# Loading input weights as whole rows, u by another queue, and a filter turned by TensorE

## The chip, the cores and the metric

The kernel runs on one core of a Trainium2 chip. A core has five engines that run side by side, each through its own list of instructions in order: PE (TensorE, matmuls, with PEld for its weight loads), DVE (VectorE), ACT (ScalarE), POOL (GpSimd) and SP (SyncE, which here only issues DMAs). Sixteen DMA engines move data. The metric is the device time of one execution in microseconds (us).

## The reference

```python
for t in range(S):                       # r, k, v, w: batch 4, heads 8, S = 768, D = 48
    cur = einsum('bhd,bhe->bhde', u[None] * kt, vt)
    y[:, :, t] = einsum('bhd,bhde->bhe', rt, state + cur)
    state = wt[:, :, :, None] * state + einsum('bhd,bhe->bhde', kt, vt)
x = y as [batch, S, 384]
h = maximum(x @ w_in, 0)                 # w_in 384 x 1024, float64
conv_out[t] = sum_k conv_w[k] * h[t + k - 1]
out = (h * sigmoid(conv_out)) @ w_out    # w_out 1024 x 384, float64
```

w_in, conv_w and w_out are given in float64. [...]

## The kernel before

**Two halves.** The recurrence is computed in 24 chunks of 128 time steps (six for each batch). For a chunk, `stage_a` loads w, k, r and v (1024 runs of 192 bytes each), turns them with PE, forms running products of w with two scans on DVE (L549 and L556), and `stage_b` makes scores on PE (L660), masks them on DVE (L664), adds the carried state and writes a slice of x (`xT`) as a high and a low part. Chunks below `EARLY` = 4 move their last rows with selecting matmuls (`gather`, L569), later ones with small DMAs (L577). The second half, `block`, takes 384 time steps: 8 tiles of x @ w_in (L753, nine matmuls each), the filter and the sigmoid (`gating`), and the product with w_out (L782).

**Weights.** A slot of raw words is loaded into a tile `gh` and converted piece by piece by `convert`: four DVE instructions (`from_double`, L436, L441, L444, L447), with an ACT activation (L439) between the first and the second, a POOL product (L450), an ACT cast to the high part (L456) and a POOL subtraction for the low part (L457). A slot of w_in is a third of the columns of all three row groups: `win_pieces` (L472, L476) fills 48 and 16 partitions at a time, from runs of 3 KB or 2 KB. The filter conv_w is loaded as 3072 runs of 8 bytes, so that each channel lies in its partition. u is one row, loaded by SP behind the first four loads, spread over the partitions by a matmul with ones (L509) and copied into `ubc` by ACT.

**Order.** All of it is written as operations with an engine, a rank, the buffers they hold and a length (`LEN`, `moves`). `Plan.issue` plays these lengths through and writes each engine's instructions in the order that comes out; on the chip every engine then follows its list strictly. `Kind` says how many of the eight PSUM banks a use may hold (`pa` turned inputs and picked rows, `pb` scores and states, `mm` and `mo` the two products, `wx` conversion). Ahead of the plan stand some instructions in code order: `WARM` matmuls on a tile `junk`, memsets, tables.

Of the kernel before, what the change touches and what calls it, by code (L numbers as in the profile page):

```python
# [12 lines left out]
I32 = mybir.dt.int32  # L13
# [8 lines left out]
GH = 5  # L22
WARM = 10

CHUNK, LEAD, UNIT, DOWN, PIECE = 14.0, 0.0, 5.0, 1.6, 4.0
FIRST_IN, FIRST_OUT = 10.0, 60.0
AHEAD, GUARD = 10.0, 10.0
SPREAD = (3, 5)
EARLY = 4
COLD = 60.0  # L30


# [264 lines left out]
def rwkv_conv_moe_kernel(  # L297
# [36 lines left out]


    junk = fconst.tile([P, H, D], BF16, name="junk")
    nc.vector.memset(junk, 0.0)
    idle = junk.rearrange("p h d -> p (h d)")
    for _ in range(WARM):
# [48 lines left out]
    store = (list(banks), [])  # L388
    pa, pb, mm, mo, wx = Kind(3, store, 1), Kind(5, store, 2), Kind(3, store, 1), Kind(3, store, 1), Kind(4, store, 1)

# [18 lines left out]
    g_k = kind("g", 2, [P, HB])  # L409
    wide = ([fconst.tile([P, HB], F32, name=f"wide{i}") for i in range(4)], [])  # L410
    val_k, e_k = Kind(3, wide, 1), Kind(2, wide, 1)
# [10 lines left out]

    def from_double(raw, val, n, reads, writes):

        e, x, y = Buf(e_k), Buf(wx), Buf(wx)

        def exps():
            return x.t.bitcast(I32)[:, 0:n]

        def mant():  # L430
            return y.t.bitcast(I32)[:, 0:n]
# [28 lines left out]
    def load_conv():  # L460
        raw = Buf(conv_k)
        op("SP", "issue", lambda: nc.sync.dma_start(
            out=raw.t.rearrange("p (j t w) -> p j t w", j=3, w=2),
            in_=conv_w.rearrange("j (t p w) -> p j t w", p=P, w=2)), [], [(raw, 0)], [raw], moves=0.2)
        from_double(lambda: raw.t, lambda: cw.rearrange("p j t -> p (j t)"), 3 * FT, [raw, (raw, 0)], ["cw"])

    def win_pieces(f0, n, piece):

        raw = Buf(raw_k)
        cs = slice(2 * f0, 2 * (f0 + n))  # L470
        for g in range(2):
# [4 lines left out]
            op("SP", "issue", lambda g=g: nc.sync.dma_start(  # L476
                out=raw.t[64 * g + D:64 * g + 64, :, 0:2 * n],
                in_=w_in[(6 + g) * D:(7 + g) * D, cs].rearrange("(m i) c -> i m c", m=KT)), [], [(raw, 2 * g + 1)], [raw],
                moves=2.3 * n / 1024)
# [17 lines left out]
    def loads(n):  # L497
# [29 lines left out]
    def stage_a(n):  # L527
# [319 lines left out]
    for t0 in range(0, FT, 3):  # L847
        plan.rank = FIRST_OUT + PIECE * t0
        wout_pieces(t0, min(3, FT - t0), piece)
    blocks = [(b, s0) for b in range(B) for s0 in range(0, S, HB)]  # L850
    bi = 0
    for n in range(N + 1):
        if n < N:
            plan.rank = CHUNK * n - LEAD - AHEAD
            loads(n)
            plan.rank = CHUNK * n - LEAD
            stage_a(n)
            plan.rank = CHUNK * (n + 0.5) - LEAD
            stage_b(n)
# [50 lines left out]
```

## Time and profile before

| | us |
|---|---|
| median of 3 runs (lowest, highest) | 385.2 (384.16, 385.79) |
| the profiled execution | 383.74 |
| its span, first to last instruction | 382.0 |
| PE busy | 353.0 (92%) |
| DVE busy | 285.7 (75%) |
| ACT busy | 234.9 (61%) |
| POOL busy | 174.3 (46%) |

All rows further down are of the profiled execution. Its own time is 1.7 us above its span, and 1.5 us below the median. A busy share is a mean over the whole span; the stages differ, so the rows give them apart.

### The profile page before, as it was taken

The numbers are of one execution on the slowest core, as the hardware profiler recorded it, in microseconds if no ns is written. First come the engines' busy times: TensorE is split into PE (matmuls) and PEld (weight loads), VectorE is DVE, ScalarE is ACT, GpSimd is POOL, SyncE is SP. The second block draws the span as 40 slices with busy tenths as digits, with TensorE's granted clock in tenths as the row PEclk, the third lists the DMA queues.
The fourth block names the chain that finished last, engine by engine and source line by source line (L and its number), as shares of the span: only waits on it lengthen the run. The fifth ranks groups of instructions, "written<-read, shape, count | busy, mean of one in ns | idle before, by whom it ended". The sixth has DMA issues, their size and how long they took to land.

```text
span 382.0 us, 7869 instructions
## 1 busy us (share of the span) xinstructions
PE 353.0 (92%) x2794; PEld 322.2 (84%) x2794; DVE 285.7 (75%) x575; ACT 234.9 (61%) x612; POOL 174.3 (46%) x199
## 2 busy tenths in 40 slices
PE   6839578898899999999999999999999999999994
PEld 3728557787699999998999989998999998999993
DVE  1668999999987986778787786768879755863640
ACT  5145646898766763498648652696775625765741
POOL 5536758857854343066533450373543410332430
PEclk9977698999999999999999999999999999999998
DMA  8989993524433443543343253824334121010001
GB/s 162 129 151 172 267 241 82 115 50 79 82 75 69 100 102 53 133 98 82 74 92 85 55 106 75 165 51 99 78 85 82 33 51 57 0 44 21 22 22 66
DMA packets 116623, 34.44 MB, mean 90 GB/s; under 512 B 106146, under 2 KB 113827, under 8 KB 116579
## 3 DMA queue, kind: packets, MB, share of 16 engines
q1 hardware_dynamic: 116578, 33.89, 43.0%
q8 instruction: 23, 0.38, 0.4%
q14 instruction: 22, 0.17, 0.2%
HBM read 25.19 MB, written 4.72 MB: 78 GB/s over the span
## 4 chain that ended last, share of the span: by engine, by line
PE 73%; DVE 14%; DMA 3%; issue 3%; SPq 2%; POOL 2%; ACT 1%; DVEq 0%; POOLq 0%
PE bank L782 26%; PE bank L753 24%; PE bank L660 5%; PE bank L542 5%; PE bank L726 5%; PE bank L716 4%; DMA gh<-in_moe_w_in_dram 2%; PE bank L677 2%; PE bank L595 2%; SPq L502 1%; DVE kr L549 1%; DVE kr L556 1%; DVE wide L447 1%; DVE bank L444 1%; DVE bank L436 1%
## 5 line engine op out<-in xcount | busy, mean ns | idle before, releaser
L753 PE MATMUL bank<-xT,wi 128*128 128x386 f32 x576 | 124.5, 346 | 0.0
L782 PE MATMUL bank<-wo,gh 128*128 128x384 f32 x576 | 123.3, 343 | 0.0
L775 POOL TENSOR_TENSOR gh<-g,gh 128x384 fp32r<-128x384 f32 x64 | 64.5, 1013 | 111.3 <-ACT gh L774 105.9
L753 PEld LDWEIGHTS bank<-xT,wi 128*128 128x128 f32 x576 | 100.3, 189 | 2.9 <-issue 2.2
L782 PEld LDWEIGHTS bank<-wo,gh 128*128 128x128 f32 x576 | 99.5, 188 | 1.7 <-issue 0.9
L767 DVE SCALAR_TENSOR_TENSOR a<-bank,cw,a 128x384 f32<-128x384 f32 x64 | 38.2, 609 | 22.6 <-ACT a L766 22.6
L587 POOL TENSOR_SCALAR_AFFINE_SELECT pm<-dg 128x1024 f32<-128x1024 f32 x24 | 26.4, 1099 | 51.0 <-PE bank L726 44.8
L771 ACT ACTIVATE a<-a 128x384 f32<-128x384 f32 x64 | 33.4, 523 | 21.9 <-DVE a L769 21.7
L772 DVE TENSOR_TENSOR g<-bank,a 128x384 f32<-128x384 f32 x64 | 34.6, 547 | 11.3 <-ACT a L771 10.6
L765 ACT ACTIVATE bank<-bank 128x386 f32<-128x386 f32 x64 | 30.4, 476 | 20.3 <-PE bank L753 19.0
L664 DVE COPY_PREDICATED pm<-upper,bank 128x512 f32<-128x512 int32 x48 | 33.3, 726 | 10.5 <-PE bank L660 10.3
L769 DVE SCALAR_TENSOR_TENSOR a<-bank,cw,a 128x384 f32<-128x384 f32 x64 | 38.2, 609 | 0.6
L774 ACT CAST gh<-g 128x384 fp32r<-128x384 f32 x64 | 32.3, 511 | 9.7 <-DVE g L772 9.4
L766 ACT ACTIVATE a<-bank,cw 128x384 f32<-128x384 f32 x64 | 36.2, 579 | 0.4
L549 DVE TENSOR_TENSOR_SCAN kr<-bank,one_end 128x387 f32<-128x387 f32 x24 | 23.0, 957 | 15.9 <-PE bank L542 15.8
L581 POOL TENSOR_TENSOR z<-r,k 128x384 f32<-128x384 f32 x24 | 24.3, 1012 | 14.0 <-DMA r<-in_r_dram 14.0
L583 POOL TENSOR_TENSOR z<-z,ubc 128x384 f32<-128x384 f32 x24 | 24.3, 1011 | 4.3 <-ACT ubc L511 3.2
L660 PEld LDWEIGHTS bank<-kr 48*128 48x128 f32 x288 | 19.9, 202 | 6.7 <-issue 4.6
L660 PE MATMUL bank<-kr 48*128 48x128 f32 x288 | 24.7, 305 | 0.4 <-DVE g L772 0.4
L812 ACT COPY wide<-bank 128x384 f32<-128x384 f32 x24 | 11.5, 480 | 21.9 <-PE bank L782 21.4
L569 PE MATMUL bank<-kr,sel 128*112 128x130 f32 x48 | 10.9, 386 | 14.2 <-DVE kr L554 7.0
L556 DVE TENSOR_TENSOR_SCAN kr<-bank,dA 128x387 f32<-128x387 f32 x24 | 22.8, 952 | 0.0
(106 smaller groups left out, 542.2 us busy)
## 6 DMA issues: line engine op xcount, KB each, us to landing
w<-in_w_dram SPq DMA_DIRECT2D x24, 192.0 KB, 3.4
k<-in_k_dram SPq DMA_DIRECT2D x24, 192.0 KB, 3.5
r<-in_r_dram SPq DMA_DIRECT2D x24, 192.0 KB, 3.8
v<-in_v_dram SPq DMA_DIRECT2D x24, 192.0 KB, 3.5
out_dram<-wide SPq DMA_DIRECT2D x24, 192.0 KB, 2.0
gh<-in_moe_w_out_dram SPq DMA_DIRECT2D x2, 1152.0 KB, 9.2
last<-kr SPq DMA_DIRECT2D x120, 16.2 KB, 1.8
gh<-in_moe_w_in_dram SPq DMA_DIRECT2D x4, 432.0 KB, 7.2
```

Source lines behind the costliest of these rows:

```text
L660: nc.tensor.matmul(sc[g].t[:, m * L:(m + 1) * L], lhsT=kt(m)[p], rhs=rt(m)[p], start=True, stop=True)
L664: op("DVE", "cp", lambda g=g: nc.vector.copy_predicated(out=pm.t[:, g], mask=upper.unsqueeze(1).to_broadcast([P, NP, L]), data=sc[g].t.rea ...
L753: nc.tensor.matmul(t.t[:, 0:HB + 2], lhsT=wi[:, m, a, f * P:(f + 1) * P], rhs=xT[:, x0 + m, c, xs], start=(m == 0 and j == 0), stop=(m == ...
L765: ("ACT", "relu", lambda: nc.scalar.activation(out=h(0, width + 2), in_=h(0, width + 2), func=AF.Relu), [t], [t]),
L766: ("ACT", "mul", lambda: nc.scalar.mul(out=a(), in_=h(1), mul=cw[:, 1, bass.ds(f, 1)]), [t, "cw"], [a1]),
L767: ("DVE", "stt", lambda: nc.vector.scalar_tensor_tensor(out=a(), in0=h(0), scalar=cw[:, 0, bass.ds(f, 1)], in1=a(), op0=ALU.mult, op1=ALU. ...
L769: ("DVE", "stt", lambda: nc.vector.scalar_tensor_tensor(out=a(), in0=h(2), scalar=cw[:, 2, bass.ds(f, 1)], in1=a(), op0=ALU.mult, op1=ALU. ...
L771: ("ACT", "sig", lambda: nc.scalar.activation(out=a(), in_=a(), func=AF.Sigmoid), [], [a1]),
L772: ("DVE", "gate", lambda: nc.vector.tensor_tensor(out=g.t[:, 0:width], in0=h(1), in1=a(), op=ALU.mult), [t, a1], [g]),
L774: ("ACT", "cast", lambda: nc.scalar.copy(out=part(0)[:, 0:width], in_=g.t[:, 0:width]), [g], [key]),
L775: ("POOL", "lo", lambda: nc.gpsimd.tensor_tensor(out=part(1)[:, 0:width], in0=g.t[:, 0:width], in1=part(0)[:, 0:width].bitcast(F32), op=AL ...
L782: nc.tensor.matmul(acc.t[:, 0:DM], lhsT=part(a)[:, tt * P:(tt + 1) * P], rhs=wo[:, f, c, :], start=(f == 0 and a + c == 0), stop=(f == FT ...
```

## The change

The change does several things at once:

- u is loaded by ACT's queue as its first instruction, into a fixed tile, and its matmul stands in code order behind the junk matmuls, of which there are 5 and no longer 10. The copy into `ubc` stands in chunk 0's `stage_a`.
- A slot of w_in is one row group `m` with all 1024 columns: 128 whole rows of 8 KB, again to 48 and 16 partitions at a time, cut into pieces of 384, 384 and 256 columns for `convert`. The slots are written among the chunks' operations (slot n behind `stage_a(n)`), as are the slots of w_out.
- The filter is loaded as 24 rows of 1 KB, converted in 24 partitions, turned by one PE transpose and copied into `cw` by ACT.
- `pa` may hold 4 banks instead of 3; the picked rows and the turned keys of the first four chunks go to `pb`. Planning lengths of the weight loads and the ranks of the pieces change.

```diff
-WARM = 10
-
-CHUNK, LEAD, UNIT, DOWN, PIECE = 14.0, 0.0, 5.0, 1.6, 4.0
+WARM = 5
+
+CHUNK, LEAD, UNIT, DOWN, PIECE = 14.0, 0.0, 5.0, 1.6, 5.0
...
+CAPS = (4, 5, 3, 3, 4)
+GT, TB = 1, 1
+WIN = 2.0
...
+    wide = ([fconst.tile([P, HB], F32, name=f"wide{i}") for i in range(4)], [])
+    nc.scalar.dma_start(out=wide[0][0][0:1, :], in_=u.rearrange("h d -> (h d)").unsqueeze(0))
...
     ubc = fconst.tile([P, H, D], F32, name="ubc")
+    nc.tensor.matmul(banks[-1][:, 0:H * D], lhsT=ones_f[0:1, :], rhs=wide[0][0][0:1, :], start=True, stop=True)
...
-    pa, pb, mm, mo, wx = Kind(3, store, 1), Kind(5, store, 2), Kind(3, store, 1), Kind(3, store, 1), Kind(4, store, 1)
+    pa, pb, mm, mo, wx = (Kind(cap, store, keep) for cap, keep in zip(CAPS, (1, 2, 1, 1, 1)))
...
     def load_conv():
-        raw = Buf(conv_k)
+
+        rows = 3 * FT
+        raw, val, t = Buf(e_k), Buf(val_k), Buf(wx)
         op("SP", "issue", lambda: nc.sync.dma_start(
-            out=raw.t.rearrange("p (j t w) -> p j t w", j=3, w=2),
-            in_=conv_w.rearrange("j (t p w) -> p j t w", p=P, w=2)), [], [(raw, 0)], [raw], moves=0.2)
-        from_double(lambda: raw.t, lambda: cw.rearrange("p j t -> p (j t)"), 3 * FT, [raw, (raw, 0)], ["cw"])
-
-    def win_pieces(f0, n, piece):
+            out=raw.t.bitcast(I32)[0:rows, 0:2 * P], in_=conv_w.rearrange("j (t c) -> (j t) c", t=FT)), [], [(raw, 0)], [raw], moves=0.2)
+        from_double(lambda: raw.t.bitcast(I32)[0:rows, 0:2 * P], lambda: val.t[0:rows, 0:P], P, [raw, (raw, 0)], [val], rows)
+        op("PE", "tr", lambda: nc.tensor.transpose(out=t.t[:, 0:rows], in_=val.t[0:rows, 0:P], identity=ident[0:rows, 0:rows]),
+           [val], [t])
+        op("ACT", "fill", lambda: nc.scalar.copy(out=cw.rearrange("p j t -> p (j t)"), in_=t.t[:, 0:rows]), [t], ["cw"])
+
+    def win_pieces(m, piece):
 
         raw = Buf(raw_k)
-        cs = slice(2 * f0, 2 * (f0 + n))
...
         for g in range(2):
             op("SP", "issue", lambda g=g: nc.sync.dma_start(
-                out=raw.t[64 * g:64 * g + D, :, 0:2 * n],
-                in_=w_in[0:6 * D, cs].rearrange("(m g i) c -> g i m c", m=KT, g=2)[g]), [], [(raw, 2 * g)], [raw],
-                moves=6.9 * n / 1024)
...
-        for m in range(KT):
+                out=row()[64 * g:64 * g + D, 0:2 * DF], in_=w_in[(2 * m + g) * D:(2 * m + g + 1) * D, :]),
+                [], [(raw, 2 * g)], [raw], moves=WIN * 0.75)
+            r0 = (6 + g) * D + 16 * m
+            op("SP", "issue", lambda g=g, r0=r0: nc.sync.dma_start(
+                out=row()[64 * g + D:64 * g + 64, 0:2 * DF], in_=w_in[r0:r0 + 16, :]),
+                [], [(raw, 2 * g + 1)], [raw], moves=WIN * 0.25)
+        for f0 in range(0, DF, HB):
             plan.rank = next(piece)
...
-            [], [(raw, 0)], [raw], moves=2.3 * n)
+            [], [(raw, 0)], [raw], moves=0.95 * n)
...
-    def spread_u():
-        t, row = Buf(pa), Buf(val_k)
-        op("SP", "issue", lambda: nc.sync.dma_start(out=row.t[0:1, :], in_=u.rearrange("h d -> (h d)").unsqueeze(0)),
-           [], [row], moves=0.05)
...
-            gt = Buf(pa)
+            gt = Buf((pa, pb, mm, mo)[GT])
...
+        if n == 0:
+            op("ACT", "kh", lambda: nc.scalar.copy(out=ubc.rearrange("p h d -> p (h d)"), in_=banks[-1][:, 0:H * D]),
+               [(K_, 1)], ["ubc"])
...
-        tb = Buf(pa)
+        tb = Buf((pa, pb, mm, mo)[TB] if n < EARLY else pa)
...
-    plan.rank = -AHEAD + 1
-    spread_u()
-    for f0 in range(0, DF, HB):
-        plan.rank = FIRST_IN + PIECE * KT * (f0 // HB)
-        win_pieces(f0, min(HB, DF - f0), piece)
-        if f0 == 0:
-            load_conv()
...
             stage_a(n)
+
+            if n < KT:
+                plan.rank = FIRST_IN + PIECE * KT * n
+                win_pieces(n, piece)
+                if n == 0:
+                    load_conv()
+            if n == KT - 1:
+                for t0 in range(0, FT, 3):
...
```

Because the plan decides the order, these edits move instructions on every engine. Three places matter here. Numbers behind a name tell buffers apart and differ between the two kernels without meaning; line numbers of the changed kernel are a few higher.

**SP, the first DMAs.** These are SP's rows 4 to 15 before: the last load of chunk 0 (v), u, chunk 1's four loads, the first slot of w_in, the filter, and the first load of chunk 2.

```order
L502 DMA v_127<-in_v_dram 128x8x48
L507 DMA wide_169<-in_u_dram 1x384
L502 DMA w_122<-in_w_dram 128x8x48
L502 DMA k_124<-in_k_dram 128x8x48
L502 DMA r_126<-in_r_dram 128x8x48
L502 DMA v_128<-in_v_dram 128x8x48
L472 DMA gh<-in_moe_w_in_dram 48x3x768
L476 DMA gh<-in_moe_w_in_dram 16x3x768
L472 DMA gh<-in_moe_w_in_dram 48x3x768
L476 DMA gh<-in_moe_w_in_dram 16x3x768
L462 DMA conv_176<-in_moe_conv_w_dram 128x24x2
L502 DMA w_121<-in_w_dram 128x8x48
```

In the changed kernel the rows from the last load of chunk 1 on read:

```order
L514 DMA v_129<-in_v_dram 128x8x48
L484 DMA gh<-in_moe_w_in_dram 48x2048
L488 DMA gh<-in_moe_w_in_dram 16x2048
L484 DMA gh<-in_moe_w_in_dram 48x2048
L488 DMA gh<-in_moe_w_in_dram 16x2048
L514 DMA w_122<-in_w_dram 128x8x48
```

u and the filter are gone from this place. The filter now stands inside the third slot, behind the loads of chunk 3:

```order
L514 DMA v_128<-in_v_dram 128x8x48
L484 DMA gh<-in_moe_w_in_dram 48x2048
L488 DMA gh<-in_moe_w_in_dram 16x2048
L470 DMA wide_75<-in_moe_conv_w_dram 24x256
L484 DMA gh<-in_moe_w_in_dram 48x2048
L488 DMA gh<-in_moe_w_in_dram 16x2048
```

**PE, the first matmuls.** Before: the last of the ten junk matmuls, u's matmul, then chunk 0's turned w, k and r, its picked rows and its turned keys.

```order
L340 LDWEIGHTS junk
L340 MATMUL bank_71<-junk 128x384
L509 MATMUL bank_64<-wide_169,ones_f 128x384
L542 MATMUL bank_65<-ident,w_121 128x128 x3
L542 MATMUL bank_66<-ident,k_123 128x128 x3
L542 MATMUL bank_67<-ident,r_125 128x128 x3
L569 MATMUL bank_68<-kr_134,sel 112x130 x6
L595 MATMUL bank_69<-ident,kr_134 128x128 x3
```

The changed kernel, from the last of its five junk matmuls:

```order
L347 LDWEIGHTS junk
L347 MATMUL bank_71<-junk 128x384
L363 MATMUL bank_71<-wide_72,ones_f 128x384
L546 MATMUL bank_64<-ident,w_122 128x128 x3
L546 MATMUL bank_65<-ident,k_124 128x128 x3
L546 MATMUL bank_66<-ident,r_126 128x128 x3
L573 MATMUL bank_68<-kr_135,sel 112x130 x6
L602 MATMUL bank_69<-ident,kr_135 128x128 x3
```

The order is the same, with five junk matmuls fewer ahead of u's.

**DVE, the first conversions.** Before, from chunk 0's masking on: a conversion (`gh`) starts between chunk 0's state and chunk 1's turned k (the TENSOR_TENSOR into `kr`), and chunk 0's slice of x is written among four conversion instructions.

```order
L664 COPY_PREDICATED pm_155<-upper,bank_71 128x512
L664 COPY_PREDICATED pm_155<-upper,bank_64 128x512
L683 COPY s_163<-bank_66 112x192
L436 TENSOR_SCALAR bank_69<-gh 128x384
L444 TENSOR_SCALAR bank_70<-gh 128x384
L554 TENSOR_TENSOR kr_135<-bank_65,kr_135 128x3x128
L447 SCALAR_TENSOR_TENSOR wide_170<-gh,bank_70 128x384
L441 SCALAR_TENSOR_TENSOR wide_171<-gh,bank_69 128x384
L436 TENSOR_SCALAR bank_71<-gh 128x384
L709 TENSOR_TENSOR xT<-bank_68,xT 128x3x128
L444 TENSOR_SCALAR bank_64<-gh 128x384
L441 SCALAR_TENSOR_TENSOR wide_172<-gh,bank_71 128x384
```

The changed kernel at the same place:

```order
L671 COPY_PREDICATED pm_156<-upper,bank_70 128x512
L671 COPY_PREDICATED pm_156<-upper,bank_71 128x512
L690 COPY s_164<-bank_64 112x192
L558 TENSOR_TENSOR kr_136<-bank_65,kr_136 128x3x128
L564 TENSOR_TENSOR kr_136<-bank_66,kr_136 128x3x128
L442 TENSOR_SCALAR bank_69<-gh 128x384
L450 TENSOR_SCALAR bank_67<-gh 128x384
L591 TENSOR_REDUCE dg_155<-z_153 128x4x2
L447 SCALAR_TENSOR_TENSOR wide_72<-gh,bank_69 128x384
L453 SCALAR_TENSOR_TENSOR wide_73<-gh,bank_67 128x384
L716 TENSOR_TENSOR xT<-bank_68,xT 128x3x128
L442 TENSOR_SCALAR bank_71<-gh 128x384
```

Chunk 1's two products into `kr` now stand ahead of the first conversion instruction. The filter's four conversion instructions have left this region for the place behind the first scan of chunk 3.

## Rows read from the trace of the kernel before

**Rows 1.** the chain, start and us: the nine turning matmuls of chunk 8

```profile
111.31 0.98 PE bank L542 x9
```

**Rows 2.** stages: busy us (instructions) by engine, granted clock, DMA share, GB/s

```profile
9.18:20.00 10.82, 9.66 (x74) 8.01 (x74) 7.90 (x15) 1.89 (x8) 5.14 (x5) 1.00 1.14 128
20.00:40.00 20.00, 11.62 (x110) 9.96 (x104) 15.32 (x35) 11.47 (x35) 11.39 (x13) 0.74 1.03 168
40.00:103.00 63.00, 52.48 (x433) 45.66 (x435) 62.87 (x134) 44.45 (x122) 46.88 (x50) 0.92 0.56 129
103.00:373.00 270.00, 269.80 (x2151) 252.54 (x2152) 198.04 (x383) 170.55 (x432) 105.14 (x104) 1.00 0.33 72
373.00:382.00 9.00, 3.47 (x20) 3.15 (x19) 0.00 (x0) 1.44 (x3) 0.00 (x0) 0.81 0.20 70
```

**Rows 3.** chain and timelines (start, us): u, first scan, picked rows

```profile
3.57 2.93 DMA wide<-in_u_dram
...
6.63 1.61 PE L509 MATMUL bank<-wide,ones_f 1*128 1x384 f32 x2 [2.06 <-DMA wide<-in_u_dram]
8.18 0.90 PE L542 MATMUL bank<-ident,w 128*128 128x128 f32 x3
...
9.18 0.96 DVE L549 TENSOR_TENSOR_SCAN kr<-bank,one_end 128x387 f32<-128x387 f32 x1 [6.63 <-PE bank L542]
...
12.85 1.64 PE bank L569 x6
```

**Rows 4.** ACT's timeline: the copy that waits for chunk 0's w

```profile
3.63 0.27 ACT L536 COPY w<-w 128x96 f32<-128x96 f32 x1 [1.31 <-DMA w<-in_w_dram]
```

**Rows 5.** what DVE waited for, 9 to 45 us: us in total, times, longest

```profile
DVE kr L549 <- PE bank L542: 6.6, 1, 6.6
DVE dg L584 <- POOL z L583: 2.7, 1, 2.7
DVE wide L441 <- ACT bank L439: 2.4, 3, 1.7
DVE xT L709 <- ACT xT L708: 1.2, 1, 1.2
DVE bank L436 <- DMA gh<-in_moe_w_in_dram: 0.9, 1, 0.9
```

**Rows 6.** timeline, 10 to 35 us: SP's blocked load and who waits behind it

```profile
10.40 8.41 SPq L502 DMA_DIRECT2D w<-in_w_dram  x1
...
19.60 0.56 DVE L436 TENSOR_SCALAR bank<-gh 128x384 int32<-128x384 int32 x1
21.17 0.27 ACT L536 COPY w<-w 128x96 f32<-128x96 f32 x1 [5.43 <-DMA w<-in_w_dram]
25.02 0.47 ACT L708 CAST xT<-bank 128x384 fp32r<-128x384 f32 x1
30.21 1.65 PE L660 MATMUL bank<-kr 48*128 48x128 f32 x12
```

**Rows 7.** DMA packets in 2.5:9.8, 10.5:16.5, 16.8:19.6 and 44:48.4 us

```profile
DMA packets 8007, 1.56 MB, mean 213 GB/s; under 512 B 7992, under 2 KB 7993, under 8 KB 8007
DMA packets 383, 0.99 MB, mean 164 GB/s; under 512 B 62, under 2 KB 62, under 8 KB 383
DMA packets 3050, 0.07 MB, mean 26 GB/s; under 512 B 3036, under 2 KB 3036, under 8 KB 3050
DMA packets 591, 1.78 MB, mean 404 GB/s; under 512 B 16, under 2 KB 16, under 8 KB 590
```

**Rows 8.** DVE's conversion by shape: count | busy us, mean ns | idle

```profile
L441 DVE SCALAR_TENSOR_TENSOR wide<-gh,bank 128x384 int32<-128x384 int32 x14 | 7.7, 547 | 2.2 <-ACT bank L439 2.1
L441 DVE SCALAR_TENSOR_TENSOR wide<-gh,bank 128x256 int32<-128x256 int32 x3 | 1.2, 410 | 0.0
L436 DVE TENSOR_SCALAR bank<-conv 128x24 int32<-128x24 int32 x1 | 0.2, 178 | 0.0
```

**Rows 9.** PE's timeline: the same twelve score matmuls later on

```profile
57.52 0.94 PE L660 MATMUL bank<-kr 48*128 48x128 f32 x12
```

More of the change, by code (lines that the diff above doesn't have):

```diff
@@ L409, in rwkv_conv_moe_kernel @@
     g_k = kind("g", 2, [P, HB])
-    wide = ([fconst.tile([P, HB], F32, name=f"wide{i}") for i in range(4)], [])
     val_k, e_k = Kind(3, wide, 1), Kind(2, wide, 1)
@@ L420, in rwkv_conv_moe_kernel, with from_double @@
     fast.enter_context(tc.manual_schedule())
-    def from_double(raw, val, n, reads, writes):
+    def from_double(raw, val, n, reads, writes, rows=P):
         e, x, y = Buf(e_k), Buf(wx), Buf(wx)
         def exps():
-            return x.t.bitcast(I32)[:, 0:n]
+            return x.t.bitcast(I32)[0:rows, 0:n]
         def mant():
-            return y.t.bitcast(I32)[:, 0:n]
+            return y.t.bitcast(I32)[0:rows, 0:n]
         def word(i):
@@ L438, in from_double @@
             reads, [x])
-        op("ACT", "exp", lambda: nc.scalar.activation(out=exps(), in_=exps(), func=AF.Relu, scale=2.0 ** 23, bias=ebias),
-           [], [x])
+        op("ACT", "exp", lambda: nc.scalar.activation(
+            out=exps(), in_=exps(), func=AF.Relu, scale=2.0 ** 23, bias=ebias[0:rows]), [], [x])
         op("DVE", "wstt", lambda: nc.vector.scalar_tensor_tensor(
-            out=e.t.bitcast(I32)[:, 0:n], in0=word(1), scalar=-2 ** 31, in1=exps(), op0=ALU.bitwise_and, op1=ALU.bitwise_or),
+            out=e.t.bitcast(I32)[0:rows, 0:n], in0=word(1), scalar=-2 ** 31, in1=exps(), op0=ALU.bitwise_and, op1=ALU.bitwise_or),
             [*reads, x], [e])
@@ L449, in from_double @@
             [*reads, y], writes)
-        op("POOL", "lo", lambda: nc.gpsimd.tensor_tensor(out=val(), in0=val(), in1=e.t[:, 0:n], op=ALU.mult),
-           [e], writes, port=True)
+        op("POOL", "lo", lambda: nc.gpsimd.tensor_tensor(
+            out=val(), in0=val(), in1=e.t[0:rows, 0:n], op=ALU.mult), [e], writes, port=True)
     def convert(raw, hi, lo, n, reads, token):
@@ L469, in win_pieces, with row @@
+        from_double(lambda: raw.t.bitcast(I32)[0:rows, 0:2 * P], lambda: val.t[0:rows, 0:P], P, [raw, (raw, 0)], [val], rows)
[3 more added lines that the diff above has]
+    def win_pieces(m, piece):
         raw = Buf(raw_k)
-        cs = slice(2 * f0, 2 * (f0 + n))
+        def row():
+            return raw.t.rearrange("p j c -> p (j c)")
@@ L471, in win_pieces @@
         for g in range(2):
             op("SP", "issue", lambda g=g: nc.sync.dma_start(
-                out=raw.t[64 * g:64 * g + D, :, 0:2 * n],
-                in_=w_in[0:6 * D, cs].rearrange("(m g i) c -> g i m c", m=KT, g=2)[g]), [], [(raw, 2 * g)], [raw],
-                moves=6.9 * n / 1024)
[L476 to L479, printed above, removed]
@@ L480, in win_pieces @@
-        for m in range(KT):
+                out=row()[64 * g:64 * g + D, 0:2 * DF], in_=w_in[(2 * m + g) * D:(2 * m + g + 1) * D, :]),
[5 more added lines that the diff above has]
+        for f0 in range(0, DF, HB):
             plan.rank = next(piece)
-            convert(lambda m=m: raw.t[:, m, 0:2 * n], wi[:, m, 0, f0:f0 + n], wi[:, m, 1, f0:f0 + n], n,
+            n = min(HB, DF - f0)
+            convert(lambda f0=f0, n=n: row()[:, 2 * f0:2 * (f0 + n)], wi[:, m, 0, f0:f0 + n], wi[:, m, 1, f0:f0 + n], n,
@@ L503, in loads @@
                 out=st[nm].t[:, :, 0:D], in_=src[b, :, s, :].rearrange("h t d -> t h d")), [], [st[nm]], moves=1.15)
-    def spread_u():
-        t, row = Buf(pa), Buf(val_k)
-        op("SP", "issue", lambda: nc.sync.dma_start(out=row.t[0:1, :], in_=u.rearrange("h d -> (h d)").unsqueeze(0)),
-           [], [row], moves=0.05)
-        op("PE", "gather", lambda: nc.tensor.matmul(t.t[:, 0:H * D], lhsT=ones_f[0:1, :], rhs=row.t[0:1, :],
-                                                    start=True, stop=True), [row], [t])
-        op("ACT", "kh", lambda: nc.scalar.copy(out=ubc.rearrange("p h d -> p (h d)"), in_=t.t[:, 0:H * D]), [t], ["ubc"])
     def seg(t, at):
@@ L839, in rwkv_conv_moe_kernel @@
     piece = iter([FIRST_IN + PIECE * j for j in range(3 * KT)] + [FIRST_OUT + PIECE * j for j in range(FT)])
-    plan.rank = -AHEAD + 1
-    spread_u()
-    for f0 in range(0, DF, HB):
-        plan.rank = FIRST_IN + PIECE * KT * (f0 // HB)
-        win_pieces(f0, min(HB, DF - f0), piece)
-        if f0 == 0:
-            load_conv()
-    for t0 in range(0, FT, 3):
-        plan.rank = FIRST_OUT + PIECE * t0
-        wout_pieces(t0, min(3, FT - t0), piece)
     blocks = [(b, s0) for b in range(B) for s0 in range(0, S, HB)]
@@ L857, in rwkv_conv_moe_kernel @@
             stage_a(n)
+            if n < KT:
[5 more added lines that the diff above has]
+                for t0 in range(0, FT, 3):
+                    plan.rank = FIRST_OUT + PIECE * t0
+                    wout_pieces(t0, min(3, FT - t0), piece)
             plan.rank = CHUNK * (n + 0.5) - LEAD
```

1 line of the change is left out of this document (removed).

## The prediction

> **What bounds the kernel now.** I read the stages first [rows 2]. From 103 to 373 us PE is busy for 269.80 of 270.0 us: this stage is as long as its matmuls, 270 us, and nothing that waits for memory or another engine shows. Its granted clock is 1.00. From 40 to 103 us it is DVE that has no gap (62.87 of 63.0 us), while PE idles for 10.5 us: the chunks' scans, the conversion of the weights and the first gating all queue there. Before 40 us neither is full. So the end is set by a chain of three: when DVE's queue begins, how long it idles until it is full, and then its work until PE has products enough. The last 9 us are the drain of the last block; the tail of the order on PE, DVE, ACT and SP is the same in both kernels.
>
> A shift in DVE's queue reaches the end in full if the work on both sides of it is the same. I counted both orders at chunk 8's turned w, which lies at 111.3 us [rows 1], when PE is full: ahead of it stand in both kernels 99 matmuls of the first product and 33 of the second, and all conversions are done on DVE ahead of its scan, with ten first filter steps (L767) in both. What is left for PE is thus equal, and the time at the end moves by as much as this point does.
>
> Where DVE idles, then. It does not start until 9.18 us [rows 3]. Then it idles for 2.92 us up to 20 us and 4.68 us from 20 to 40 us, and 0.13 us after that [rows 2]. By name [rows 5]: 2.7 us for chunk 1's z, 2.4 us in three waits for the exponent step on ACT, 1.2 us for ACT's cast of chunk 0's x, 0.9 us for a slot of w_in.
>
> **The start.** u is SP's fifth DMA: issued at 3.57 us, landed 2.93 us later [rows 3]. PE's queue holds u's matmul at its head, so it waits until 6.63 us, works 1.61 us on u, then turns chunk 0's w, and the scan follows at 9.18 us: 2.55 us from u's matmul to the scan. But w had landed at 3.63 us, and ACT's copy of it was done at 3.9 us [rows 4]. In the changed kernel u is ACT's first instruction. I let it be issued at 0.82 us, as SP's first load is, and take the same 2.93 us: u's matmul at 3.9 us, the scan at 6.45 us, **2.7 us earlier**. Bounds: the copy of w at 3.9 us leaves 0.9 us to turn it, so the scan cannot come before 4.9 us (4.3 us gained); were u as late as 5 us, 1.5 us are left. The copy into `ubc` goes ahead of chunk 0's copy of r on ACT; it comes earlier with u, and what it feeds (z and the diagonal) is wanted only after the scores, so I price its place at nothing.
>
> Against it stands an exchange in DVE's order: chunk 0's second scan now comes ahead of its k product. The first six picked-row matmuls start with that product, so they no longer run beside the second scan, and all twelve stand in a row. Six took 1.64 us [rows 3], of which they lose what the scan hid, some 0.7 us (bounds 0 and 1.6): **0.7 us lost**. The wait for chunk 1's turned w behind it stays (2.92 us, of which 2.7 us are now charged to z).
>
> **The loads.** One chunk's load is 1024 packets; 7992 packets went in 7.3 us, 0.93 us a load [rows 7]. The eight loads of chunks 0 and 1 are through at about 9.9 us. Then a slot of w_in: 321 packets of 3 KB in 6.0 us, 164 GB/s. Then the filter: its 3072 runs of 8 bytes hold all engines for 2.8 us at 26 GB/s. Chunk 2's w sits behind both; SP needs 8.41 us to issue it [rows 6]. ACT then waits 5.43 us for it, and behind that copy stand the exponent step and the cast of x that DVE waits for. That is 1.7 of the 2.4 us, the 1.2 us and, one slot later, the 0.9 us.
>
> The change takes away the 2.8 us; 24 rows of 1 KB replace them. The slot goes from 1.18 to 1.05 MB, in rows of 8 KB. Its rate shows in no row: 164 GB/s for w_in's own runs to 48 and 16 partitions, 404 GB/s for w_out's 3 KB runs to 128 partitions [rows 7]. Both are 3 KB runs, so the run's length is not what parts them; the partitions stay as they were, and I take 164 GB/s, 6.4 us a slot (at 404 it is 2.6 us). [...]
>
> At 164 GB/s: first slot through at 16.3 us, chunk 2 at 20.0, second slot 26.4, chunk 3 at 30.1, half the third slot 33.3, and 0.9 us until seen. DVE's first conversion comes 10.4 us after its first scan today (19.60 us, [rows 6]); with chunk 1's two products now ahead of it, 6.45 + 10.4 + 0.9 = 17.8 us, and the slot is there at 17.2. Chunk 2's w is there at 18.1 us instead of 21.17, and ACT's exponent step now stands ahead of its copy. So the waits on ACT and the slot go. In their place DVE comes to the filter's conversion some 14 us of work after the first one, with 1 us of waits at 32.8 us; the filter is there at 34.2 us: 1.5 us waited, with the matmul operands of chunk 3 queued behind it. At 404 GB/s it lies there at 25 us. I leave 1.0 us for waits in DVE's order that I can't place. So 2.5 us of idle stand for 4.68: **2.2 us gained** (bounds 0 and 4.7).
>
> **The rest.** The filter's DVE instructions become 128 wide in 24 partitions: between 178 ns and 410 ns each [rows 8], at 280 ns 0.4 us for four; they stand where DVE waits for the filter's slot anyway, and would cost that without it. Conversion of w_in has the same six pieces of 384 and three of 256 columns. One more PE transpose (under 0.3 us) and an ACT copy lie in PE's 8.4 us of gaps from 20 to 40 us [rows 2]. Five junk matmuls less end before u lands. Bank limits and new planning lengths move instructions after 111 us; PE's stage there has no idle to give, and I price it at nothing, since DVE has 72 us to spare in it, ACT 99 us and POOL 165 us [rows 2]; the bad case is a rival.
>
> **Sum.** 2.7 − 0.7 + 2.2 = 4.2 us. The profiled 383.74 us becomes 379.5 us; it is 1.5 us below the median of the runs, so against 385.2 I say **381.0 us**. Bounds added up: 1.5 − 1.6 + 0 = 0 and 4.3 − 0 + 4.7 = 9.0 us; as these won't all meet, the forecast's own range is 378.5 to 383.3. Half a per cent, 1.9 us, is about what a measurement of this kernel can tell from no change.
>
> **The rivals.** *The rows come at w_out's rate.* The filter's wait goes (1.5 us), and u, alone in front, lands at 2.9 us: 0.9 us more. 4.2 + 2.4 = 6.6 us, 378.6 us; with the unplaced waits gone too, 377. For it speaks that w_in's runs skip 5 KB in every 8 KB of the source while w_out's lie end to end; against it the partitions.
>
> *The start is gained and lost again at PE's low clock.* The same twelve score matmuls take 1.65 us at 30.21 us and 0.94 us at 57.52 [rows 6, 9]; granted clock 0.74 in the stage from 20 to 40 us [rows 2], a mix of 1.2 and 2.4 GHz, with 8.4 us of gaps. That stage's 11.62 us of matmuls at 0.74 would be 17.2 us at the low level, 5.6 more; two thirds of it I put in the chain (picked rows, scores, turned inputs): 3.7 of the 4.2 us, 384.7 us. Against it: with fewer gaps I expect the clock high sooner. The Trainium skill's "TensorE: Matmul & The Clock Gate" ("Part 1: The HAM clock gate") has activity release the clock; five junk matmuls fewer speak for this rival.
>
> *Slower: PE waits in its long stage.* With `pa` at 4 of eight banks and other lengths, the order may starve the products of banks. 16 chunks follow chunk 7; 0.26 us of PE idle in each eats the gain, 0.38 us makes the kernel slower by over half a per cent, and 0.5 us gives 389 us. Against it: PE's 0.2 us of idle in 270 today, beside engines with much slack.
>
> **How the numbers follow.** Forecast 0.52, rows at the high rate 0.22, eaten 0.15, slower 0.11. Faster by over 0.5%: nearly all of the first two, 0.74; within 0.5%: 0.16; slower 0.10. The range goes from the second case's end, 376.5, to no change, 385.0, and leaves out the slower case and some of the high.
>
> **What would show it.** The first scan near 6.5 us; u's matmul near 3.9 us. The slot's packets at 164 or 404 GB/s. DVE's idle from 20 to 40 us down to about 2.5 us, and the wait at the filter. Chunk 8's turned w near 107 us, and PE without idle from there to its end near 369 us. Wrong would be: a first scan after 8 us, new waits of DVE for weights between 30 and 60 us, or PE idle in its long stage.

## The result and the profile after

The changed kernel takes 381.98 us (median of 12 runs, 380.08 to 384.24), the kernel before 384.52 us on the same chip. The ratio is 0.9943, interval 0.9919 to 0.9967: about 2.2 us faster, where 4.2 us were forecast. The profiled run of after took 381.53 us with a span of 379.8 us, 2.2 us less than before.

The timeline of after at the start (start us, us, what; in brackets the idle time ahead and what ended it) answers to [rows 3]:

```profile
0.82 0.51 ACTq L340 DMA_DIRECT2D wide<-in_u_dram  x1
...
2.91 1.64 PE L363 MATMUL bank<-wide,ones_f 1*128 1x384 f32 x2
...
4.49 0.90 PE L546 MATMUL bank<-ident,w 128*128 128x128 f32 x3
...
5.49 0.96 DVE L553 TENSOR_TENSOR_SCAN kr<-bank,one_end 128x387 f32<-128x387 f32 x1 [2.95 <-PE bank L546]
```

u's matmul no longer waits behind SP's queue, and the first scan comes 3.69 us earlier than in [rows 3]. The stages of after, in the columns of [rows 2]:

```profile
9.18:20.00 10.82, 10.10 (x96) 8.69 (x94) 6.91 (x14) 3.27 (x14) 3.90 (x4) 1.00 1.06 187
20.00:40.00 20.00, 16.14 (x139) 13.86 (x140) 16.73 (x38) 10.01 (x35) 12.09 (x14) 0.75 1.02 173
40.00:103.00 63.00, 50.23 (x391) 42.26 (x389) 59.41 (x127) 45.82 (x124) 46.95 (x49) 0.92 0.49 119
103.00:371.00 268.00, 268.00 (x2133) 251.74 (x2132) 193.39 (x383) 169.02 (x427) 105.21 (x104) 1.00 0.33 72
```

PE (first) is ahead at 40 us and full from 103 us on. But DVE (third), which had 0.13 us of idle from 40 to 103 us [rows 2], now has 3.59 us there. What it waited for from 20 to 103 us (us in total, times, longest):

```profile
DVE wide L447 <- ACT bank L445: 2.8, 4, 2.0
DVE bank L442 <- DMA wide<-in_moe_conv_w_dram: 2.0, 1, 2.0
DVE xT L740 <- ACT xT L738: 1.0, 1, 1.0
DVE kr L558 <- DVE dA L557: 0.5, 1, 0.5
DVE bank L551 <- PE bank L546: 0.5, 1, 0.5
```

The first two lie close together. The timeline of after, 30 to 43 us:

```profile
30.15 0.39 SPq L514 DMA_DIRECT2D w<-in_w_dram  x1
...
35.40 0.28 DVE L442 TENSOR_SCALAR bank<-wide 24x128 int32<-24x128 int32 x1 [1.99 <-DMA wide<-in_moe_conv_w_dram]
...
39.83 0.27 ACT L540 COPY w<-w 128x96 f32<-128x96 f32 x1 [2.92 <-DMA w<-in_w_dram]
...
41.44 0.55 ACT L445 ACTIVATE bank<-bank,ebias 128x384 int32<-128x384 int32 x1
42.02 0.55 DVE L447 SCALAR_TENSOR_TENSOR wide<-gh,bank 128x384 int32<-128x384 int32 x1 [1.98 <-ACT bank L445]
```

DVE waits for the filter's rows at 33.4 us. Then ACT waits 2.92 us for chunk 4's w, which SP issued at 30.15 us behind the third slot of w_in. Behind that copy, in ACT's order, stands the exponent step that DVE needs at 40.0 us. In the chain, chunk 8's turned inputs lie here:

```profile
109.54 0.98 PE bank L546 x9
```

That is 1.77 us ahead of [rows 1], most of the 2.2 us at the end.

### The profile page after: what moved, and what is told of

It reads as the page before. It is cut to its first block, busy times and chain, and to the rows that moved or that the text cites. A ratio compares the mean times of both kernels' runs of the same rounds, so it can differ in the third digit from the quotient of the medians.

```text
span 379.8 us, 7861 instructions
## 1 busy us (share of the span) xinstructions
PE 354.3 (93%) x2790; PEld 323.0 (85%) x2790; DVE 281.5 (74%) x575; ACT 235.0 (62%) x613; POOL 174.9 (46%) x199
## 4 chain that ended last, share of the span: by engine, by line
PE 74%; DVE 9%; DMA 6%; issue 4%; ACT 3%; POOL 2%; SPq 1%; DVEq 0%; POOLq 0%
PE bank L789 26%; PE bank L760 24%; PE bank L733 5%; PE bank L667 5%; PE bank L546 4%; PE bank L723 4%; DMA r<-in_r_dram 4%; PE bank L684 2%; DMA k<-in_k_dram 2%; PE bank L602 2%; DMA wide<-in_moe_conv_w_dram 1%; DVE wide L447 1%; DVE g L779 1%; DVE a L774 1%; POOL wide L456 1%
## 5 line engine op out<-in xcount | busy, mean ns | idle before, releaser
L789 PE MATMUL bank<-wo,gh 128*128 128x384 f32 x576 | 125.7, 345 | 2.0 <-POOL wo L463 1.0
L778 ACT ACTIVATE a<-a 128x384 f32<-128x384 f32 x64 | 33.3, 522 | 27.0 <-DVE a L776 27.0
L671 DVE COPY_PREDICATED pm<-upper,bank 128x512 f32<-128x512 int32 x48 | 33.4, 725 | 8.5 <-PE bank L667 8.4
L773 ACT ACTIVATE a<-bank,cw 128x384 f32<-128x384 f32 x64 | 36.5, 580 | 0.6
L588 POOL TENSOR_TENSOR z<-r,k 128x384 f32<-128x384 f32 x24 | 24.3, 1014 | 19.6 <-DMA r<-in_r_dram 19.6
L667 PEld LDWEIGHTS bank<-kr 48*128 48x128 f32 x288 | 18.7, 189 | 6.9 <-issue 4.5
L667 PE MATMUL bank<-kr 48*128 48x128 f32 x288 | 23.7, 291 | 0.5 <-DVE wide L453 0.4
L733 PE MATMUL bank<-pm,v 128*48 128x128 f32 x320 | 22.3, 282 | 0.0
```

The costliest lines, as they stand in the source:

```text
L667: nc.tensor.matmul(sc[g].t[:, m * L:(m + 1) * L], lhsT=kt(m)[p], rhs=rt(m)[p], start=True, stop=True)
L671: op("DVE", "cp", lambda g=g: nc.vector.copy_predicated(out=pm.t[:, g], mask=upper.unsqueeze(1).to_broadcast([P, NP, L]), data=sc[g].t.rea ...
L733: nc.tensor.matmul(y.t[rows, cs], lhsT=vf[:, h * D:h * D + rows.stop - rows.start], rhs=pm.t[:, g, m, :], start=(c == 0 and m == 0), stop= ...
L773: ("ACT", "mul", lambda: nc.scalar.mul(out=a(), in_=h(1), mul=cw[:, 1, bass.ds(f, 1)]), [t, "cw"], [a1]),
L778: ("ACT", "sig", lambda: nc.scalar.activation(out=a(), in_=a(), func=AF.Sigmoid), [], [a1]),
L789: nc.tensor.matmul(acc.t[:, 0:DM], lhsT=part(a)[:, tt * P:(tt + 1) * P], rhs=wo[:, f, c, :], start=(f == 0 and a + c == 0), stop=(f == FT ...
```

## The experiments

All ratios are to the kernel before on the same chip, with 95% intervals. Where two changed kernels are compared in us, their medians can come from two chips; the kernel before took 384.17 to 384.52 us on these.

**u alone.** The kernel before, with only u's new way:

```diff
-WARM = 10
+WARM = 5
+    nc.scalar.dma_start(out=wide[0][0][0:1, :], in_=u.rearrange("h d -> (h d)").unsqueeze(0))
+    nc.tensor.matmul(banks[-1][:, 0:H * D], lhsT=ones_f[0:1, :], rhs=wide[0][0][0:1, :], start=True, stop=True)
-    spread_u()
```

> The kernel before with only the new way of u (ACT's queue, the matmul right behind five warm-up matmuls, a fixed tile); slots, filter and banks as before. Ramp theory (what the start gains is given back while the rows of w_in come, because the loads of 10 to 40 us stay where they were): first scan at 5.5 us, but the time falls by less than 1 us, to 383.5 to 384.5. Start theory (the start's gain reaches the end): first scan at 5.5 us and about 3 us gained, 381.5.

380.64 us, 0.9912 (0.9879 to 0.9945): 3.65 us below the 384.29 us of before beside it. Its first scan is at 5.49 us. One part of the change alone gives as much as the whole, as far as these runs can tell: the 1.3 us by which it is ahead lie within the two intervals. The start's gain does reach the end in the old order, and the ramp theory as I wrote it falls for that kernel.

**A later start.** The changed kernel with 15 warm-up matmuls:

```diff
-WARM = 5
+WARM = 15
```

> The changed kernel with 15 warm-up matmuls in place of 5, so that u's matmul and the first scan come about 3.6 us later, near where they were before (9.1 us), with every engine's order unchanged behind them. Ramp theory: the delay is taken up by the waits for loads between 10 and 40 us, and the time rises by less than 1 us over that of the changed kernel (382 to 383). Start theory: it rises by 2 to 3.6 us, to 384 to 385.5, and the whole change is worth nothing without it.

382.56 us, 0.9962 (0.9933 to 0.9991). The first scan lies at 7.39 us, so 1.9 us were taken away, not 3.6; the time rose by 0.6 us, which the intervals don't part from nothing, nor from the 1.9 us. The trace decides. DVE comes to the filter's conversion without a wait, and starts it when the changed kernel did (35.40 us):

```profile
35.41 0.26 DVE L442 TENSOR_SCALAR bank<-wide 24x128 int32<-24x128 int32 x1
```

So the wait for the filter has taken up the whole delay. Chunk 8's turned w lies at 109.14 us, in the changed kernel at 109.38. In the changed kernel these 1.9 us of the start do not reach the end. The test is not quite clean behind this point: here chunk 4's w was copied at 37.36 us already and not at 39.83; why the loads were ahead isn't shown.

**The filter first.** The changed kernel, its 24 rows on ACT's queue into a gating tile:

```diff
+    filt = g_k.places[1][0:3 * FT, 0:2 * P].bitcast(I32)
+    nc.scalar.dma_start(out=filt, in_=conv_w.rearrange("j (t c) -> (j t) c", t=FT))
-        op("SP", "issue", lambda: nc.sync.dma_start(
+        op("SP", "issue", lambda: None, [], [(raw, 0)], [raw], moves=0.2)
```

> The changed kernel with the filter's 24 rows loaded by ACT's queue at the start, into a gating tile that is free until about 57 us; orders of all engines unchanged but for the one issue on SP. Ramp theory: the 2.0 us wait of DVE at 33.4 us goes, but chunk 4's w still lands near 39.8 us and the exponent on ACT behind it still holds DVE there, so of 2.0 us at most 1 reaches the end: 381 to 382. Rival (the filter's wait passes to the end in full): 380. Rival (PE alone sets the end): 382.

381.74 us, 0.9926 (0.9895 to 0.9958): no change that can be told. Its timeline shows where the 2.0 us went:

```profile
38.72 0.27 ACT L541 COPY w<-w 128x96 f32<-128x96 f32 x1 [3.05 <-DMA w<-in_w_dram]
...
42.01 0.55 DVE L449 SCALAR_TENSOR_TENSOR wide<-gh,bank 128x384 int32<-128x384 int32 x1 [3.21 <-ACT bank L447]
```

The filter's wait is gone, DVE comes to the next wait earlier, waits 3.21 us there in place of 1.98, and leaves it at 42.01 us, as after did at 42.02. Chunk 4's w takes up what was won ahead of it. (The profiled execution, 383.17 us, is the slowest of the nine; I read it only up to this point.) The same in the other direction shows in the run on ACT's order further down, whose edit first acts at 82 us: there DVE waits 4.18 us for the filter, and still leaves the next wait at the same time.

```profile
36.77 0.28 DVE L446 TENSOR_SCALAR bank<-wide 24x128 int32<-24x128 int32 x1 [4.18 <-DMA wide<-in_moe_conv_w_dram]
...
41.95 0.55 DVE L451 SCALAR_TENSOR_TENSOR wide<-gh,bank 128x384 int32<-128x384 int32 x1 [0.55 <-ACT bank L449]
```

**128 partitions in a transfer.** The changed kernel, a slot by two transfers:

```diff
-                out=row()[64 * g:64 * g + D, 0:2 * DF], in_=w_in[(2 * m + g) * D:(2 * m + g + 1) * D, :]),
+                out=row()[:, g * DF:(g + 1) * DF], in_=w_in[P * m:P * (m + 1), g * DF:(g + 1) * DF]),
-            op("SP", "issue", lambda g=g, r0=r0: nc.sync.dma_start(
+            op("SP", "issue", lambda: None,
```

> The changed kernel, with each slot of w_in loaded as 128 consecutive rows by two DMAs of 128 partitions x 4 KB in place of four of 48, 16, 48 and 16 partitions x 8 KB; the rows of w_in then stand in another order than those of x, so the product is another one, and the work is the same. Orders unchanged. Theory that the few partitions of a DMA hold the rows at 160 to 195 GB/s: the packets of 10 to 17 us go at 300 to 400 GB/s, DVE's waits at 33.4 and 40.0 us (2.0 us each) go, and the time falls to 378 to 380. Rival (the rows' rate is w_in's own, or the many small packets of the chunks hold the queue): rate and time stay, 381.5 to 382.5.

376.73 us, 0.9806 (0.9765 to 0.9848): 5.2 us below the changed kernel, the largest effect of the study, with every engine's order but SP's the same. The packets from 10.5 to 13 us, when most bytes are a slot's, in the changed kernel:

```profile
DMA packets 84, 0.46 MB, mean 184 GB/s; under 512 B 28, under 2 KB 28, under 8 KB 28
```

and here:

```profile
DMA packets 430, 0.74 MB, mean 297 GB/s; under 512 B 260, under 2 KB 260, under 8 KB 430
```

DVE's wait for the filter is gone, L447's waits for the exponent are 0.8 us in place of 2.8, and from 14 to 56 us ACT waits for no chunk's w. The stages, as in [rows 2]:

```profile
20.00:40.00 20.00, 16.15 (x167) 13.53 (x163) 19.39 (x44) 13.01 (x43) 14.48 (x17) 0.91 0.96 236
40.00:103.00 63.00, 52.68 (x396) 44.63 (x397) 61.37 (x130) 46.77 (x123) 46.20 (x48) 0.92 0.42 97
```

DVE's idle from 20 to 103 us falls from 6.86 us in the changed kernel to 2.24 us, which is most of the 5.2 us.

**The rungs from u alone.** First the filter in 24 rows on top of u alone, with load_conv and from_double as in the change:

```diff
-    conv_k = kind("conv", 1, [P, 6 * FT], I32)
-        raw = Buf(conv_k)
+        raw, val, t = Buf(e_k), Buf(val_k), Buf(wx)
+        op("PE", "tr", lambda: nc.tensor.transpose(out=t.t[:, 0:rows], in_=val.t[0:rows, 0:P], identity=ident[0:rows, 0:rows]),
```

> The kernel before with u first and the filter in 24 rows turned by PE; w_in's slots stay column slices, banks as before. It is the second rung from the kernel with u alone (380.6 us). If the filter's 3,072 small runs cost anything there, the packets of 16 to 24 us go faster and it is 1 to 2 us faster, 379 to 380; if the exchange of rows and the turn only shift the order, 380 to 381.5; if the in-order wait for the filter's rows is what the whole change loses against u alone, it is slower, 382.

383.01 us, 0.9972 (0.9940 to 1.0004): 2.4 us worse than u alone, with intervals that just touch. Then that filter loaded first, by the edit above:

> The kernel with u first and the filter in 24 rows (383.0 us), with those rows loaded by ACT's queue at the start; orders of the engines as there but for the one issue on SP. Theory that the in-order wait for the filter's rows (2.1 us of DVE at 31.9 us) is what the filter costs over u alone (380.6 us): the wait goes and the time comes back to 380.5 to 381.5. Theory that the order around the filter's own operations costs it (DVE's later waits of 60 to 110 us, PE's low clock after them): it stays at 382.5 to 383.5, as taking the same wait away changed nothing in the changed kernel.

383.41 us, 0.9984 (0.9959 to 1.0010), an interval wholly above that of u alone. So the filter in rows costs the kernel with u first some 2.4 to 2.8 us, and the wait for its rows is not the reason. From 40 to 70 us the two read, in the columns of [rows 2]:

```profile
40.00:70.00 30.00, 19.99 (x141) 17.96 (x142) 27.67 (x62) 18.31 (x53) 23.79 (x26) 0.72 0.66 177
40.00:70.00 30.00, 20.64 (x148) 18.33 (x149) 28.13 (x63) 19.39 (x57) 24.92 (x27) 0.72 0.63 169
```

With u alone PE is busy for 24.98 us there at a clock of 0.85, and DVE for 29.90. So the loss shows in PE's and DVE's work after 40 us, whether the filter's rows are waited for or not; which place of the order makes it isn't shown. Next the slots as whole rows too, with the change's planning lengths, which is the changed kernel with the old banks:

```diff
-CAPS = (4, 5, 3, 3, 4)
-GT, TB = 1, 1
+CAPS = (3, 5, 3, 3, 4)
+GT, TB = 0, 0
```

> The changed kernel with the picked rows and the turned-back keys in the banks of the kernel before, and its old limits. If the bank picks are what the whole change loses against u alone, 380 to 381; if the slots as whole rows are, it stays at 381.5 to 383.

382.79 us, 0.9953 (0.9922 to 0.9984). Neither the whole rows (from 383.01) nor the new banks (to 381.98) is a step that these runs can tell from nothing, and the banks are not what loses the gain.

**Two queues.** The changed kernel, g = 1 of each slot issued by ACT:

```diff
-            op("SP", "issue", lambda g=g: nc.sync.dma_start(
+            op("SP", "issue", lambda g=g: (nc.sync, nc.scalar)[g].dma_start(
```

> The changed kernel, with the two transfers of each slot for partitions 64 to 127 issued by ACT in place of SP, so that rows for both halves of the partitions are under way at once; the other orders unchanged. If the few partitions in flight hold the rate, the packets of 10 to 20 us go from 181 to some 240 GB/s as with 128 partitions, and the time falls to 378 to 380. If the transfers of a queue already overlap, the rate stays at 180 and the time at 381.5 to 382.5; ACT's six issues of about 0.5 us each are then a small loss.

382.99 us, 0.9965 (0.9934 to 0.9996), and 177 GB/s from 10 to 20 us where the changed kernel has 187. A second queue does not lift the rate. The Trainium skill says in "DMA: Bandwidth & Descriptors", section "Issuing engines are not separate DMA queues", that transfers run on the same 16 DMA engines, whichever engine issued them. The rate here agrees.

**128 partitions, short runs.** u alone, with its column slices to 128 partitions:

```diff
-                out=raw.t[64 * g:64 * g + D, :, 0:2 * n],
-                in_=w_in[0:6 * D, cs].rearrange("(m g i) c -> g i m c", m=KT, g=2)[g]), [], [(raw, 2 * g)], [raw],
+                out=raw.t[:, :, g * n:(g + 1) * n],
+                in_=w_in[:, 2 * f0 + g * n:2 * f0 + (g + 1) * n].rearrange("(m p) c -> p m c", p=P)), [], [(raw, 2 * g)], [raw],
```

> The kernel before with u first, and each of w_in's column slices loaded by two DMAs of 128 partitions in place of four of 48 and 16 (rows in another order than x, so another product; the same work; orders unchanged). If the number of partitions is what holds w_in's rate in both layouts, it gains about 4 to 5 us over u alone, as the changed kernel did (382.0 to 376.7): 376 to 377. If the length of the runs matters too (here 1.5 KB and 1 KB), it gains less: 378 to 380.

378.26 us, 0.9828 (0.9790 to 0.9867): 2.4 us below u alone, half of what I expected if partitions alone count, and inside the range that I had named for the case in which the length of the runs matters too. The rate, from 10.5 to 13 us:

```profile
DMA packets 860, 0.90 MB, mean 361 GB/s; under 512 B 273, under 2 KB 860, under 8 KB 860
```

Runs of 1.5 KB at 361 GB/s beside rows of 8 KB at 184: the rate follows the partitions, not the length of a run, and so the length does not explain the smaller gain. What does isn't shown; u alone had less to win, since its DVE idles for 3.1 us from 20 to 103 us, after 6.9 in the changed kernel.

**ACT's order at 82 us.** In after PE waits 2.34 us at 84.19 us for a copy on ACT (L659) that stands behind three others. The edit moves the two copies (operations 521 and 522) up in the finished order, right behind the one that makes sd (520):

```diff
+        for i, behind in ((521, 520), (522, 521)):
+            entry = next(x for x in order if x[1] == i)
+            order.remove(entry)
+            order.insert(next(j for j, x in enumerate(order) if x[1] == behind) + 1, entry)
         self.order = order
```

> The changed kernel, with one pair of ACT's operations in another place: the two copies of the scaled state (sbd) for which PE waits 2.34 us at 84.2 us go ahead of a cast of w_out, a cast of gh and a relu, right behind the operation that makes sd. Everything else stands as it was. Theory of the new order (what the start gains is given back at 70 to 103 us, where the changed order makes PE wait and its clock fall): PE's wait falls from 2.3 to about 0.9 us, the clock of 80 to 90 us may rise from 0.83, and the time falls by 1 to 3 us, to 379 to 381. Theory that the loads of 10 to 40 us decide: 381.5 to 382.5, since a later wait takes it.

383.15 us, 0.9965 (0.9939 to 0.9990). PE's wait fell to 0.96 us as expected, the clock of 80 to 90 us stayed at 0.83, and nothing came at the end. The theory that this wait gives the gain back falls.

**A gather by GpSimd.** The rows in their right places, by one transfer of 128 partitions a slot:

```diff
+            nc.gpsimd.indirect_dma_start(out=row()[:, 0:2 * DF], out_offset=None, in_=w_in,
+                                         in_offset=bass.IndirectOffsetOnAxis(ap=rows_i[:, m:m + 1], axis=0))
...
-            op("SP", "issue", lambda g=g: nc.sync.dma_start(
+            op("SP", "issue", fetch if g == 0 else lambda: None, [], [(raw, 2 * g)], [raw], moves=WIN * 0.75)
```

> The changed kernel, with each slot fetched by one indirect transfer of GpSimd, a row number for each of 128 partitions (computed by GpSimd in the first microseconds), in place of SP's four transfers of 48 and 16 partitions; the right rows in the right places, the other engines' orders as they were. If the number of partitions in a transfer is what holds the rate at 160 to 195 GB/s, it goes at 250 to 350 GB/s as with 128 consecutive rows (376.7 us), and the time is 376.5 to 379. If GpSimd's issuing costs more than that gives (its queue holds z and the differences), 380 to 384.

378.50 us, 0.9833 (0.9802 to 0.9864): 3.5 us below the changed kernel. Packets from 10.5 to 13 us, and GpSimd's three issues in the timeline:

```profile
DMA packets 492, 0.96 MB, mean 385 GB/s; under 512 B 383, under 2 KB 383, under 8 KB 383
```

```profile
7.58 1.19 POOL L495 DMA_INDIRECT gh<-in_moe_w_in_dram,rows_i  x1 [0.30 <-POOL rows_i L380]
...
14.84 1.01 POOL L495 DMA_INDIRECT gh<-in_moe_w_in_dram,rows_i  x1
...
23.27 1.01 POOL L495 DMA_INDIRECT gh<-in_moe_w_in_dram,rows_i  x1
```

These are the same rows of 8 KB to the same places as in the changed kernel, at twice the rate. Partitions and the number of transfers for a slot (four, two, one) change together in these runs, so gaps between transfers are a rival. The queues from 10.5 to 13 us (packets, MB, share of the 16 engines' time), SP's in the changed kernel and then GpSimd's here, speak against it:

```profile
q1 hardware_dynamic: 84, 0.46, 106.2%
q0 software_dynamic: 109, 0.89, 94.1%
```

The engines are full in both. In the changed kernel 56 of the 84 packets are rows, and they fill as much time as 109 rows here: each row takes longer where it goes to few partitions. A run with four transfers of 128 partitions was not made.

**The gather, and ACT's order.** The last two edits together:

> Both of the former together. If the two losses are apart from each other, their gains add: 375 to 377.5. If both are the same idle time, as good as the better of the two.

378.13 us, 0.9847 (0.9818 to 0.9877): the gather's time. These two are the best versions with the reference's work.

## Why the prediction was right, and where it was not

The direction and the range held; the gain was 2.2 us where 4.2 were forecast. By its steps:

- **The start: 2.7 us forecast, 3.69 measured.** The term was too small: I gave u the 2.93 us that it took as SP's fifth transfer, and alone in front it took at most 2.1 (issued at 0.82 us, its matmul at 2.91, right behind the junk matmuls). The high case stood in a rival as 0.9 us more, and it came without that rival's rate.
- **The exchange: 0.7 us forecast.** Chunk 1's first scan lies at 12.48 us, before at 16.04, so 3.56 of 3.69 us were left: 0.13 us lost.
- **The slots: 164 GB/s taken, 184 measured**, and the first conversion waited for its slot until 17.58 us (forecast 17.2). The Trainium skill says in "SBUF — State Buffer" ("Door 1: The DMA port swizzle") that DMA bandwidth depends on how many of the 16 ports the partitions reach. The rates agree: transfers into at most 48 partitions at 184 GB/s, into 128 at 297 to 385. The ports themselves show in no run.
- **DVE's idle: the step that failed.** I forecast 2.5 us in place of 4.68 from 20 to 40 us and nothing new after. It was 3.27 us there and 3.59 us from 40 to 103 us: 2.05 us more in all, where the sum had 2.2 us less. The sentence that failed is "So the waits on ACT and the slot go." The filter's wait came as forecast (1.99 us at 33.4, forecast 1.5 at 32.8). But I followed the loads only that far, and the exponent step, which stands ahead of the copy of chunk 2's w as I wrote, stands behind that of chunk 4's. By my own rates the second half of the third slot ends at 33.3 + 3.2 = 36.5 us, with chunk 4's w behind it; it was copied at 39.83 us, and ACT's order held DVE until 42.02. The sign of being wrong that I had named, new waits of DVE for weights between 30 and 60 us, is there.
- **Sum with the measured terms:** 3.69 − 0.13 − 2.05 = 1.5 us; chunk 8's turned inputs moved by 1.77 us, the end by 2.2 us. That the time fell into the range is in part luck: the start and the exchange came out 1.6 us better than forecast, DVE's idle 4.25 us worse.
- **That a shift at chunk 8's turned w reaches the end** held, and so did PE's full stage (268.00 of 268.0 us): the slower rival is refuted.
- **Rows at w_out's rate:** refuted by the packets. Its price was right in kind: with 128 partitions the time is 376.73 us, where the rival said 378.6, or 377 with the unplaced waits gone.
- **The start lost again at PE's low clock:** not borne out. The clock of 20 to 40 us is 0.75 (before 0.74), and of DVE's waits from 20 to 103 us 0.5 us are for PE. With u alone the clock from 20 to 40 us is 0.62, lower still, and its 3.65 us reach the end all the same.

Why the start's gain reaches the end with u alone and not in the changed kernel, the stages of three kernels tell in part (columns as in [rows 2]; the profiled execution of u alone, 379.07 us, is the fastest of its seven). Before:

```profile
0.00:40.00 40.00, 27.21 (x193) 20.81 (x193) 24.74 (x59) 18.50 (x56) 22.24 (x47) 0.87 1.01 155
40.00:70.00 30.00, 23.85 (x207) 20.96 (x208) 29.94 (x68) 17.59 (x54) 20.81 (x23) 0.83 0.79 196
70.00:103.00 33.00, 28.63 (x227) 24.70 (x228) 32.93 (x67) 26.86 (x68) 26.07 (x27) 1.00 0.35 69
```

After:

```profile
0.00:40.00 40.00, 32.89 (x253) 26.20 (x254) 28.69 (x68) 18.76 (x61) 22.72 (x47) 0.87 0.98 174
40.00:70.00 30.00, 23.44 (x211) 19.56 (x209) 27.44 (x62) 19.89 (x61) 21.90 (x23) 0.88 0.74 189
70.00:103.00 33.00, 26.79 (x181) 22.70 (x180) 31.96 (x66) 25.93 (x64) 25.05 (x26) 0.95 0.27 55
```

u alone:

```profile
0.00:40.00 40.00, 29.30 (x205) 22.52 (x205) 28.33 (x67) 19.40 (x58) 23.58 (x48) 0.81 1.00 159
40.00:70.00 30.00, 24.98 (x208) 21.59 (x208) 29.90 (x68) 19.23 (x56) 22.81 (x26) 0.85 0.74 188
70.00:103.00 33.00, 29.45 (x252) 24.84 (x253) 32.90 (x67) 27.31 (x74) 24.86 (x26) 1.00 0.40 79
```

With u alone DVE gains 3.6 us of work by 40 us and then stays full. The changed kernel gains 4.0 us, gives 3.5 back in 40 to 103 us, and PE gives back 2.2 of its 5.7 us.

Shown: what is won ahead of 40 us is taken up by the waits for the filter and for chunk 4's w (the filter's wait at 0, 1.99 or 4.18 us, DVE left at 42.0 us; the start put 1.9 us later, the filter's conversion at 35.4 us as before), and with the slots at 128 partitions, where these waits are gone, 5.2 us come. Open: what in the new order costs DVE and PE their time from 70 to 103 us, and why the filter in rows costs some 2.5 us on u alone. The wait for the filter's load, the banks and the copy at 82 us were each tried and are not it; the whole order is another one, and I have not parted it further.

## What to carry to other kernels

Follow a transfer queue to its end, not to the first wait that it makes: a wait that goes ahead of a late transfer only lengthens the wait for it. Where several loads share a queue, first ask how many partitions each transfer reaches; that was worth more here (5.2 us) than any order that was tried. And when a change has parts, run the smallest alone: here u by ACT's queue gave as much as the whole, as far as the runs can tell.

## What the runs showed of the hardware

- The rate of a load followed the partitions of its transfers: rows of 8 KB went at 184 GB/s to 48 and 16 partitions, at 385 to 128 (with the chunks' packets beside them in both). With 128 partitions the rates show no order by length of the runs: 361 GB/s at 1.5 KB, 404 at 3 KB [rows 7], 297 at 4 KB, 385 at 8 KB.
- A gather of 128 rows by GpSimd takes 1.01 to 1.19 us to issue, and its rows move at 385 GB/s together with the chunks' packets, no slower than plain transfers of 128 partitions (297 and 361 GB/s).
- Behind 15 warm-up matmuls, u's two matmuls took 0.91 us, behind 5 they took 1.64; the three that turn w took 0.55 and 0.90 us. So ten more cost the first scan 1.9 us, though they alone take 3.0 us (4.78 against 1.78). Later it was the other way: behind 15, PE stood idle from 8.8 to 10.2 us, and the granted clock was 0.50 (1.2 GHz) from 11 to 15 us; behind 5 it was 1.00 (2.4 GHz) there.
